# An FFT filter with a gated FFN on one Trainium2 core: the transformed rows placed at another address, 160 bytes past the input weights mod 256

## The chip, the cores and the metric

The kernel runs on one core of one Trainium2 chip. The metric is the device time of one execution in microseconds (us), the median of repeated runs; shorter is better. A profiled execution of the same kernel gives the rows of the profile and the trace.

## The reference

Eight sequences of 3136 rows with 256 features each are filtered along the sequence in the frequency domain and then go through a gated feed-forward layer:

```python
X = np.fft.rfft(x, axis=1)                       # x: 8 x 3136 x 256
y = np.fft.irfft(X * (filt_r + 1j * filt_i), n=3136, axis=1)

h = np.maximum(y @ w_in, 0.0)                    # 256 -> 1024
conv_out[s] = sum over k of conv_w[k] * h[s + k - 1]   # 3 taps along the rows
gate = 1.0 / (1.0 + np.exp(-conv_out))
return (h * gate) @ w_out                        # 1024 -> 256
```

## The kernel before, in words

**Forward part.** A sequence of 3136 = 112 x 28 rows is transformed in stages of small float32 matmuls: `first` (line 323), a transpose through TensorE (line 334), `second` (lines 346 and 349), the filter on VectorE and GpSimd (lines 358 to 362) and `third` (line 233), whose result goes to a scratch tensor in HBM. The last inverse stage, `last_stage` (line 215), reads it back as `br` and leaves four 128x112 blocks in PSUM. `last_out` turns these into two tiles: ScalarE copies the rounded value (line 146) into `y0`, VectorE writes what the rounding left over (line 149) into `y1`. These two are the high and the low *part* of the transformed rows, in a type (float32r) that TensorE takes at a higher rate than float32.

**The tiles the change touches.** `y_slices` makes, for each sequence, two tiles `y0` and `y1` of 128 partitions x 2 x (3136 + 2) elements. Index 1 is the *half*: features 0 to 127 and 128 to 255. The two extra columns hold the zero rows at the ends, which the convolution needs. The tiles of even sequences lie in the pool `y_even`, allocated from the right end of SBUF, those of odd sequences in `y_odd`, allocated from the left behind the pool `rest`. The pool `rest` has a tile `pad` of 192 elements that nobody reads or writes; all it does is to move what is allocated behind it.

**Feed-forward part.** The schedule is written by hand: a loop over 448 steps (28 chunks of 896 rows x 8 blocks of 128 hidden features x 2 halves of a chunk of 448 rows). In each step TensorE does `inner`: 450 columns of rows (448 and one more on either side) against one block of the input weights, in three products (high weights x high rows on line 177, high x low on line 178, low x high on line 179) for each of the two halves of the features, so six matmuls of 128x450 in the order 177, 178, 179 (half 0), 177, 178, 179 (half 1). Each has its own weight load of 128x128 from `wi`. The rows are the *moving* operand, streamed through the array. Behind it comes `project` of an earlier step: 9 or 12 matmuls of 128x256 (lines 498 to 500), with the gated features `g` as the loaded weights and the output weights `wo` as the moving operand. ScalarE does relu, scaling, sigmoid and rounding (lines 465, 467, 477, 146), VectorE the taps and the product (472, 473, 478), GpSimd the low part of `g` (152). In some steps, 14 to a sequence, a piece of the next sequence's last inverse stage is put between.

**Where the operands lie** (byte offsets in a partition, and the same mod 256):

| operand | offset | mod 256 |
|---|---|---|
| `wi` high, low | 1696, 9888 | 160, 160 |
| `wo` high, low | 18080, 26272 | 160, 160 |
| `g`, all buffers | 117472 and on | 224 |
| odd `y0` / `y1`, half 0 | 60064 / 85184 | 160 / 192 |
| odd `y0` / `y1`, half 1 | 72616 / 97736 | 168 / 200 |
| even `y0` / `y1`, half 0 | 179104 / 204224 | 160 / 192 |
| even `y0` / `y1`, half 1 | 191656 / 216776 | 168 / 200 |

A block of weights starts at a multiple of 512 bytes from the tile's start, and a piece of 448 rows at a multiple of 1792 = 7 x 256, so these residues hold for every matmul of `inner`. Counted from the weights, the six matmuls read their rows at 0, 32, 0 (half 0) and 8, 40, 8 (half 1).

Of the kernel before, what the change touches and what calls it, by code (L numbers as in the profile page):

```python
# [9 lines left out]
F32 = mybir.dt.float32  # L10
F32R = mybir.dt.float32r
# [5 lines left out]
S = 3136  # L17
# [5 lines left out]
KT = D // 128  # L23
# [101 lines left out]
def tile_fft_filter_gated_ffn(  # L125
# [67 lines left out]
    ys, yps = {}, []  # L193
# [6 lines left out]

    def y_slices(b, sl):
        if sl.start == 0:
            ys[b] = [yps[b % 2].tile([128, KT, S + 2], F32R, name=f"y{h}") for h in range(2)]
            for t in ys[b]:
                nc.gpsimd.memset(t[:, :, 0:1].bitcast(F32), 0.0)
                nc.gpsimd.memset(t[:, :, S + 1:S + 2].bitcast(F32), 0.0)
        return (t[:, :, 1:S + 1].rearrange("p k (a c) -> p k c a", c=N2)[:, :, sl] for t in ys[b])
# [10 lines left out]
    def last_out(b, c):  # L218
        yh, yl = y_slices(b, slice(c, c + 2))
        pv = lasts.pop((b, c))[:, 0:4 * N1].rearrange("p (k c a) -> p k c a", c=2, a=N1)  # L220
        hi_act(yh, pv)
        lo_dve(yl, pv, yh)

    NP = 14
    rest = ctx.enter_context(tc.tile_pool(name="rest", bufs=3))
    i1_sb = rest.tile([120, G, 112], F32, name="i1_sb", bufs=1)
    rest.tile([128, 192], F32, name="pad", bufs=1)
    parts = {}

    def third(b, p, ps):  # L230
# [366 lines left out]
```

## Time and profile before

| | |
|---|---|
| time of three runs | 1559.26, 1559.91, 1562.10 us; median 1559.91 |
| profiled execution | 1559.94 us, span of its instructions 1558.2 us |
| granted TensorE clock | 0.999 |
| TensorE busy | 1537.8 us (99%) |
| VectorE, ScalarE, GpSimd busy | 1297.0, 1245.0, 703.0 us |

In the profile PE is TensorE's matmuls and PEld its weight loads, DVE is VectorE, ACT ScalarE, POOL GpSimd. A float32 matmul appears as two instructions, one for each of its passes, while a float32r one appears once. Matmuls are pipelined, so the duration shown of one is longer than the distance from its start to the next one's start; both are used below, and kept apart.

### The profile page before, as it was taken

Reading aid. Unit: us, or ns where it says so; the run is one execution under the profiler, and the core shown is the slowest. Engines: PE = TensorE matmul, PEld = TensorE weight load, DVE = VectorE, ACT = ScalarE, POOL = GpSimd, SP = SyncE. Lnnn points to the kernel's source line nnn. Section 1 sums busy time; section 2 is a strip of 40 time slices with the busy share of each in tenths; the row PEclk is TensorE's granted clock in tenths of the full one; section 3 lists DMA queues with packets and bytes.
Section 4 is the critical chain, followed back from the end, with each engine's and each line's share of the span. In section 5 each row is a group of like instructions: output and inputs, shape, how many; then the busy total and the mean of one; then the engine's idle time right before and its main releaser. Section 6 shows DMA issues by size and latency. Waiting matters only on the chain.

```text
span 1558.2 us, 27801 instructions
## 1 busy us (share of the span) xinstructions
PE 1537.8 (99%) x10320; PEld 1418.2 (91%) x10320; DVE 1297.0 (83%) x1978; ACT 1245.0 (80%) x2274; POOL 703.0 (45%) x625
## 2 busy tenths in 40 slices
PE   8999999998999999999999999999999999999998
PEld 7787778877999999999999999999999999999998
DVE  3888888788888888888888888888888888888887
ACT  5655555566888888888888888888888888888887
POOL 3455555533444444444444444444444434444444
PEclk9999999999999999999999999999999999999999
DMA  9855555452111011111111011111011110100001
GB/s 236 261 179 168 172 169 164 137 148 78 33 52 48 31 47 48 49 49 47 48 42 36 27 53 52 44 48 48 31 48 42 49 54 27 46 25 25 24 25 48
DMA packets 89062, 115.24 MB, mean 74 GB/s; under 512 B 7400, under 2 KB 60168, under 8 KB 88928
## 3 DMA queue, kind: packets, MB, share of 16 engines
q1 hardware_dynamic: 74592, 87.77, 18.4%
q10 hardware_dynamic: 14336, 25.70, 5.8%
q8 instruction: 82, 1.34, 0.4%
q14 instruction: 52, 0.43, 0.1%
HBM read 62.06 MB, written 51.38 MB: 73 GB/s over the span
## 4 chain that ended last, share of the span: by engine, by line
PE 94%; DMA 2%; DVE 1%; ACT 1%; issue 0%; SPq 0%; POOL 0%; ACTq 0%; POOLq 0%; DVEq 0%
PE ps_h L178 12%; PE ps_h L179 12%; PE ps_h L177 11%; PE po L498 11%; PE po L500 11%; PE po L499 11%; PE ps L233 6%; PE ps_h L215 5%; PE pp L346 5%; PE ps L323 5%; PE ps L334 3%; DMA x<-in_x 1%; PE ps L215 1%; DVE y L149 1%; ACT y L146 0%; PE pp L349 0%
## 5 line engine op out<-in xcount | busy, mean ns | idle before, releaser
L152 POOL TENSOR_TENSOR g<-t,g 128x448 fp32r<-128x448 f32 x448 | 517.1, 1154 | 663.5 <-ACT g L146 259.3
L498 PE MATMUL po<-wo,g 128*128 128x256 f32 x1568 | 441.4, 282 | 0.0
L500 PE MATMUL po<-wo,g 128*128 128x256 f32 x1568 | 433.9, 277 | 0.4 <-POOL g L152 0.4
L499 PE MATMUL po<-wo,g 128*128 128x256 f32 x1568 | 433.4, 276 | 0.0
L472 DVE SCALAR_TENSOR_TENSOR t<-ps_h,cw,t 128x448 f32<-128x448 f32 x448 | 305.7, 682 | 85.6 <-ACT t L467 75.2
L178 PE MATMUL ps_h<-y,wi 128*128 128x450 f32 x896 | 330.3, 369 | 5.6 <-DVE y L149 5.6
L177 PE MATMUL ps_h<-y,wi 128*128 128x450 f32 x896 | 329.1, 367 | 3.3 <-DVE t L478 1.9
L179 PE MATMUL ps_h<-y,wi 128*128 128x450 f32 x896 | 328.8, 367 | 0.0
L473 DVE SCALAR_TENSOR_TENSOR t<-ps_h,cw,t 128x448 f32<-128x448 f32 x448 | 306.5, 684 | 16.0
L467 ACT ACTIVATE t<-ps_h,cw 128x448 f32<-128x448 f32 x448 | 284.8, 636 | 43.2 <-ACT ps_h L465 2.6
L498 PEld LDWEIGHTS po<-wo,g 128*128 128x128 f32 x1568 | 294.8, 188 | 7.1
L499 PEld LDWEIGHTS po<-wo,g 128*128 128x128 f32 x1568 | 294.3, 188 | 5.7
L500 PEld LDWEIGHTS po<-wo,g 128*128 128x128 f32 x1568 | 294.5, 188 | 0.6 <-POOL g L152 0.6
L465 ACT ACTIVATE ps_h<-ps_h 128x450 f32<-128x450 f32 x448 | 251.8, 562 | 32.9 <-PE ps_h L179 27.0
L478 DVE TENSOR_TENSOR t<-ps_h,t 128x448 f32<-128x448 f32 x448 | 275.3, 615 | 0.1
L477 ACT ACTIVATE t<-t 128x448 f32<-128x448 f32 x448 | 255.0, 569 | 12.4 <-DVE t L473 11.2
L146 ACT ACTIVATE g<-t 128x448 fp32r<-128x448 f32 x448 | 254.7, 568 | 0.2 <-DVE t L478 0.2
L362 POOL TENSOR_TENSOR z<-u,v 120x512 f32<-120x512 f32 x112 | 156.6, 1398 | 184.3 <-DVE v L360 154.1
L178 PEld LDWEIGHTS ps_h<-y,wi 128*128 128x128 f32 x896 | 168.3, 188 | 14.7 <-DVE y L149 7.9
L179 PEld LDWEIGHTS ps_h<-y,wi 128*128 128x128 f32 x896 | 168.3, 188 | 13.9
L177 PEld LDWEIGHTS ps_h<-y,wi 128*128 128x128 f32 x896 | 169.9, 190 | 11.7 <-DVE t L478 2.9
L149 DVE TENSOR_TENSOR y<-ps_h,y 128x448 fp32r<-128x448 f32 x98 | 103.1, 1053 | 75.3 <-ACT y L146 75.3
(62 smaller groups left out, 1661.6 us busy)
## 6 DMA issues: line engine op xcount, KB each, us to landing
x<-in_x SPq DMA_DIRECT2D x112, 224.0 KB, 2.9
b_dram<-sb ACTq DMA_DIRECT2D x112, 224.0 KB, 2.3
br<-b_dram SPq DMA_DIRECT2D x112, 224.0 KB, 2.6
out<-ot SPq DMA_DIRECT2D x27, 896.0 KB, 4.1
raw<-in_w_in SPq DMA_DIRECT2D x8, 256.0 KB
raw<-in_w_out SPq DMA_DIRECT2D x8, 256.0 KB
t_sb<-in_fr SPq DMA_DIRECT2D x15, 112.0 KB
t_sb<-in_fi SPq DMA_DIRECT2D x14, 112.0 KB
```

The costliest lines, as they stand in the source:

```text
L152: nc.gpsimd.tensor_tensor(out=dst, in0=src, in1=hi.bitcast(F32), op=ALU.subtract)
L177: nc.tensor.matmul(ps, lhsT=wh, rhs=rh, start=start, stop=False, **kw)
L178: nc.tensor.matmul(ps, lhsT=wh, rhs=rl, start=False, stop=False, **kw)
L179: nc.tensor.matmul(ps, lhsT=wl, rhs=rh, start=False, stop=stop, **kw)
L467: nc.scalar.activation(t, h[:, 1:SUB + 1], AF.Copy, scale=cw[:, 1, f:f + 1])
L472: nc.vector.scalar_tensor_tensor(out=t, in0=h[:, 0:SUB], scalar=cw[:, 0, f:f + 1], in1=t, op0=ALU.mult, op1=ALU.add)
L473: nc.vector.scalar_tensor_tensor(out=t, in0=h[:, 2:SUB + 2], scalar=cw[:, 2, f:f + 1], in1=t, op0=ALU.mult, op1=ALU.add)
L477: nc.scalar.activation(t, t, AF.Sigmoid)
L478: nc.vector.tensor_mul(t, h[:, 1:SUB + 1], t)
L498: nc.tensor.matmul(o, lhsT=gh[:, sl], rhs=wo[0][:, f], start=first, stop=False, skip_group_check=True)
L499: nc.tensor.matmul(o, lhsT=gh[:, sl], rhs=wo[1][:, f], start=False, stop=False, skip_group_check=True)
L500: nc.tensor.matmul(o, lhsT=gl[:, sl], rhs=wo[0][:, f], start=False, stop=last, skip_group_check=True)
```

## The change

The rows' tiles get a pitch of 3136 + 64 elements for a half (12800 bytes = 50 x 256, before 12552), so that both halves and both parts start at the same residue mod 256. The pool of either kind of sequence is moved by a further 40 elements (160 bytes): on the left through the tile `pad`, on the right through a new unused tile. All four starts of the even tiles and all four of the odd ones are now at 64 mod 256, which is 160 past the input weights' 160.

```diff
     def y_slices(b, sl):
         if sl.start == 0:
-            ys[b] = [yps[b % 2].tile([128, KT, S + 2], F32R, name=f"y{h}") for h in range(2)]
+            ys[b] = [yps[b % 2].tile([128, KT, S + 64], F32R, name=f"y{h}") for h in range(2)]
+            if b < 2:
+                yps[b].tile([128, 40], F32, name="pad_y")
...
     i1_sb = rest.tile([120, G, 112], F32, name="i1_sb", bufs=1)
-    rest.tile([128, 192], F32, name="pad", bufs=1)
+    rest.tile([128, 232], F32, name="pad", bufs=1)
```

No instruction is added, removed or moved: on every engine the same instructions stand in the same order with the same waits, and only operand addresses differ. What lies behind `pad` moves along: the forward part's `z`, `sb`, `turn1`, `eye`, `s2`, `a`, `u`, `v` and the filter tiles by 160 bytes, `br` to 64 mod 256 (from 160). `wi`, `wo`, `m2`, `i1`, `s1`, `x` and `turn0` keep their addresses, and the feed-forward part's `t`, `g` and `ot` keep theirs mod 256 (224).

## Prediction

> **What bounds the kernel now.** The page first: whose time is the kernel's time. The rows are the span, part 1 (busy time) and part 4 (the chain of work that ended last, by engine).
>
> ```profile
> span 1558.2 us, 27801 instructions
> PE 1537.8 (99%) x10320; PEld 1418.2 (91%) x10320; DVE 1297.0 (83%) x1978; ACT 1245.0 (80%) x2274; POOL 703.0 (45%) x625
> ...
> PE 94%; DMA 2%; DVE 1%; ACT 1%; issue 0%; SPq 0%; POOL 0%; ACTq 0%; POOLq 0%; DVEq 0%
> ```
>
> TensorE is the kernel: 94% of the chain. The span is 1558.2 us, and the profiled execution's own time 1559.94, so 1.7 us lie around it; the median of the runs, 1559.91, is the same number. I sum against 1559.9. Next, by stretch: columns are the stretch, its length, then busy time of PE, PEld, DVE, ACT and POOL, granted clock, DMA share, GB/s.
>
> ```profile
> 0.00:365.00 365.00, 356.96 (x2132) 285.86 (x2132) 287.90 (x421) 219.45 (x379) 182.44 (x147) 1.00 0.62 180
> 365.00:1558.20 1193.20, 1180.82 (x8188) 1132.37 (x8188) 1009.08 (x1558) 1025.52 (x1895) 520.58 (x478) 1.00 0.13 41
> 380.00:960.00 580.00, 576.98 (x4026) 554.37 (x4025) 497.53 (x764) 504.97 (x931) 252.94 (x235) 1.00 0.14 44
> ```
>
> The feed-forward part is 1193 of 1558 us, at full clock, and PE is busy for 577 of 580 us. ScalarE comes next with 505 of 580, or 87%, so PE could get some 12% faster there before another engine is last. Hence a matmul that starts sooner shortens the end directly. Now the matmuls themselves, one step in the timeline (start, duration):
>
> ```profile
> 1001.69 0.37 PE L177 MATMUL ps_h<-y,wi 128*128 128x450 f32 x1
> 1001.90 0.36 PE L178 MATMUL ps_h<-y,wi 128*128 128x450 f32 x1
> 1002.10 0.37 PE L179 MATMUL ps_h<-y,wi 128*128 128x450 f32 x1
> 1002.30 0.36 PE L177 MATMUL ps_h<-y,wi 128*128 128x450 f32 x1
> 1002.51 0.37 PE L178 MATMUL ps_h<-y,wi 128*128 128x450 f32 x1
> 1002.72 0.36 PE L179 MATMUL ps_h<-y,wi 128*128 128x450 f32 x1
> 1002.92 0.28 PE L498 MATMUL po<-wo,g 128*128 128x256 f32 x1
> ...
> 1004.28 0.37 PE L177 MATMUL ps_h<-y,wi 128*128 128x450 f32 x1
> ```
>
> Six matmuls of 450 columns take 1.23 us, 205 ns from start to start; the twelve of 256 columns behind them 1.36 us, 113 ns each. Nothing stands between. So only the pace of a matmul can change the time here, and the change touches an operand of just the 450-column ones.
>
> **Does the address set that pace?** The same step in the list by line (duration ns min/median/max), each row restricted to one instruction; the order is 177, 178, 179 of half 0, then of half 1.
>
> ```profile
> L177 PE MATMUL ps_h<-y,wi x1: 367/367/367, 1001.7 to 1001.7; 128*128 128x450 f32 x1
> L178 PE MATMUL ps_h<-y,wi x1: 365/365/365, 1001.9 to 1001.9; 128*128 128x450 f32 x1
> L179 PE MATMUL ps_h<-y,wi x1: 367/367/367, 1002.1 to 1002.1; 128*128 128x450 f32 x1
> L177 PE MATMUL ps_h<-y,wi x1: 363/363/363, 1002.3 to 1002.3; 128*128 128x450 f32 x1
> L178 PE MATMUL ps_h<-y,wi x1: 369/369/369, 1002.5 to 1002.5; 128*128 128x450 f32 x1
> L179 PE MATMUL ps_h<-y,wi x1: 365/365/365, 1002.7 to 1002.7; 128*128 128x450 f32 x1
> ```
>
> With distances from the weights of 0, 32, 0, 8, 40, 8 bytes the durations are 367, 365, 367, 363, 369, 365. Lines 177 and 179 stream the very same rows, line 178 the low part. The shape, type and work are equal, and the two halves differ by 4 ns on lines 177 and 178 in opposite directions. What differs is the address (and, for the last, which operand is loaded next). Over the whole run it holds:
>
> ```profile
> L177 PE MATMUL ps_h<-y,wi x896: 363/367/579, 365.1 to 1545.1; 128*128 128x450 f32 x180
> L178 PE MATMUL ps_h<-y,wi x896: 365/369/579, 367.3 to 1545.3; 128*128 128x450 f32 x180
> L179 PE MATMUL ps_h<-y,wi x896: 360/367/579, 367.6 to 1545.5; 128*128 128x450 f32 x180
> ```
>
> 3 x 896 = 2688 matmuls, whose minimum is the fast position and whose median is the slow one on lines 177 and 178. The rows begin at seven places of each tile, 1792 bytes apart, and the blocks of weights 512 apart, and neither widens the two values: what matters, matters mod 256 or less.
>
> **How much is there to win or lose?** A matmul that streams unhindered is the lower end. The float32 passes give its price by column:
>
> ```profile
> L233 PE MATMUL ps<-z,i_sb x436: 377/378/470, 29.0 to 362.6; 120*112 120x256 f32 x146
> L346 PE MATMUL pp<-a,s_sb x208: 591/594/690, 23.1 to 360.2; 112*120 112x512 f32 x104
> L500 PE MATMUL po<-wo,g x1568: 276/276/384, 380.5 to 1553.8; 128*128 128x256 f32 x196
> ```
>
> (591 - 378) / 256 = 0.832 ns a column, and 378 - 256 x 0.832 = 165 ns of fixed latency. The float32r columns go at about twice that pace: 256 of them take 276, where 165 + 256 x 0.416 = 271.5 would be unhindered, an excess of 4.5 ns. For 450 columns it would be 165 + 187 = 352. The six positions average (367+365+367+363+369+365)/6 = 366, an excess of 14 ns, three times as much. Over 2688 matmuls that is 37.6 us: all that the address could win, with an end at 1522. Upward there is no row that bounds it; the worst position, 369, is 3 ns above the mean, or 8.1 us over all.
>
> [...]
>
> **The change part by part.** *New pitch and pads of the rows' tiles.* All six positions now read rows at one residue, 64 mod 256, 160 past the weights. The misaligned starts (168 and 200, not multiples of 16 or 32) are gone, and so is the shift of 32 between the parts. 64 isn't among the residues before, nor is 160 among the distances, so I bound the new duration: 352 from below (no hindrance), 369 as the worst seen, and from above by as much again as the mean is now hindered, 366 + 14 = 380 (+37.6 us, 1597.5). The row that is nearest in kind is line 178, half 0, at 192, the only one of the four starts that, like 64, is a multiple of 64: 365, and its successor starts 0.20 us later (1001.90 to 1002.10), where the slow 369 is followed after 0.21. The lowest row is 363, on line 177, which now also has no neighbour at another residue. I take 364, between the two: 2 ns below the mean of 366, and since durations exceed the distance between starts by a fixed amount (366 - 205 = 161), 2 ns of duration are 2 ns of time. 2688 x 2 ns = 5.4 us less, 1554.5.
>
> *Forward part, moved by 160 bytes.* Its float32 passes stream at half the pace. Line 233 loads its weights `i1` from four residues mod 256 (448 bytes a slice) against one residue of `z`, and minimum and median of 436 are 377 and 378: no address effect to 1 ns. I take nothing. If 1 ns appeared on each of its 2132 matmuls, it would be 2.1 us either way.
>
> *Writes of the rows.* ScalarE and VectorE write them in a stride of 112 bytes:
>
> ```profile
> L146 ACT ACTIVATE y<-ps_h x98: 1002/1058/1099, 389.6 to 1392.6; 128x448 fp32r<-128x448 f32 x98
> L149 DVE TENSOR_TENSOR y<-ps_h,y x98: 981/1056/1083, 390.6 to 1393.7; 128x448 fp32r<-128x448 f32 x98
> ```
>
> These hide under PE's stream (ScalarE has 13% left). Only at the seven borders between sequences, and in the 14 pieces before the feed-forward part, does TensorE wait for such a pair. Were they 10% slower, 21 x 0.2 us = 4 us at most, of which I take none: the stride stays and only the start moves.
>
> *What the new tiles cost:* nothing, since nobody touches the pads. The sum is 1559.9 - 5.4 = 1554.5.
>
> **The rivals.**
>
> *Most of the hindrance goes (faster, by far).* The 256-column matmuls read `wo` at 160 while `g` is loaded from 224, a distance of 192 bytes, near to the new 160; their excess is 4.5 ns in place of 14. If distance to the operand being loaded is what counts, the new one may come down to that: 2688 x 9.5 = 25.5 us, 1534.4. Against it: line 179 of half 1 is followed by a load of `g`, at a distance of 200, and it still takes 365. Also, in the 256-column stream a weight load may simply be the bound (PEld is busy for 554 of 580 us), so its 4.5 may tell nothing of conflicts. 0.21.
>
> *The new distance is a bad one (slower).* If the hindrance comes from rows and weights meeting in the same part of the memory while a load runs, one common residue makes all six matmuls meet it in the same way. Now they are spread over 363 to 369, then all could sit at 369 or beyond: 2688 x 3 = +8.1 us, 1568.0. It decides from a duration of 367.2 on (366 + 3.1 us / 2688). For it: 32 to 40 bytes moves it by 4 ns, so the dependence is steep, and a place picked among such values is above the mean about as often as below. Against it: half of the six positions, those on a shifted half, lose an 8-byte offset. 0.30.
>
> *Nothing happens.* The differences among the six may come from their place in the order (which product follows which) rather than from the address, and the mean stays: 1559.9. [...] 0.17.
>
> **How the numbers follow.** The forecast, a small gain near the lowest of the starts seen, has 0.32. What a measurement of this kernel can tell from no change is about 0.2%, or 3.1 us. Faster by more: the forecast and the first rival, 0.32 + 0.21 = 0.53. Same: 0.17. Slower: 0.30. Range: down to 1532, which takes in 1534.4 with the 2 us of the forward part, and leaves out the complete disappearance; up to 1571, the third of the bad cases beyond 369 left out. Cases of both signs hold most of the chance; the forecast's own range, durations from 361 to 365.5, is 1546.5 to 1558.6.
>
> **What would show it.** Right: lines 177, 178 and 179 each with one duration in the trace after (minimum and median equal, save where the next load is of another kind), near 364, and six starts of a step in 1.22 us in place of 1.23; lines 498 to 500 still 276; line 233 still 378. The first rival would show 357 and a step of 1.17 us, the second 369 or more and 1.25 us. Wrong in its ground would be: line 177 still with two values though its addresses are alike, or time that moved while these rows stood still, in the forward part (0 to 365) or as waits for lines 146 and 149.

## The result and the profile after

The changed kernel takes 1579.14 us (median of 4 runs, 1578.21 to 1579.42) against 1560.24 before: a ratio of 1.0119, 95% interval 1.0101 to 1.0136. It is 18.9 us slower, where 5.4 us less was forecast. The profiled execution took 1579.2 us.

The page after, its span, busy times and chain:

```profile
span 1577.4 us, 27801 instructions
PE 1557.2 (99%) x10320; PEld 1435.8 (91%) x10320; DVE 1295.9 (82%) x1978; ACT 1245.7 (79%) x2274; POOL 703.5 (45%) x625
...
PE 94%; DVE 2%; DMA 2%; ACT 1%; issue 0%; POOL 0%; SPq 0%; ACTq 0%; POOLq 0%; DVEq 0%
```

Nothing has taken TensorE's place: it is busy for 19.4 us more (1557.2 - 1537.8) in a span 19.2 us longer, and the others are as they were. So the same matmuls run slower. The first and last start of line 177 say where:

```profile
L177 PE MATMUL ps_h<-y,wi x896: 363/369/579, 367.3 to 1564.4; 128*128 128x450 f32 x180
```

From 367.3 to 1564.4 are 1197.1 us, before 365.1 to 1545.1, 1180.0: 17.1 of the 19.2 us lie in the feed-forward part, 2.2 ahead of it. The groups of the page, each with its count, busy time and mean duration, show which matmuls (lines 177 to 179 are the same in both kernels; `project` moved from 498-500 to 500-502). Before:

```profile
L498 PE MATMUL po<-wo,g 128*128 128x256 f32 x1568 | 441.4, 282 | 0.0
L500 PE MATMUL po<-wo,g 128*128 128x256 f32 x1568 | 433.9, 277 | 0.4 <-POOL g L152 0.4
L499 PE MATMUL po<-wo,g 128*128 128x256 f32 x1568 | 433.4, 276 | 0.0
...
L178 PE MATMUL ps_h<-y,wi 128*128 128x450 f32 x896 | 330.3, 369 | 5.6 <-DVE y L149 5.6
L177 PE MATMUL ps_h<-y,wi 128*128 128x450 f32 x896 | 329.1, 367 | 3.3 <-DVE t L478 1.9
L179 PE MATMUL ps_h<-y,wi 128*128 128x450 f32 x896 | 328.8, 367 | 0.0
```

After:

```profile
L500 PE MATMUL po<-wo,g 128*128 128x256 f32 x1568 | 445.2, 284 | 0.0
L501 PE MATMUL po<-wo,g 128*128 128x256 f32 x1568 | 438.9, 280 | 0.0
L502 PE MATMUL po<-wo,g 128*128 128x256 f32 x1568 | 437.7, 279 | 0.4 <-POOL g L152 0.4
...
L178 PE MATMUL ps_h<-y,wi 128*128 128x450 f32 x896 | 332.0, 371 | 5.6 <-DVE y L149 5.6
L177 PE MATMUL ps_h<-y,wi 128*128 128x450 f32 x896 | 333.3, 372 | 3.2 <-DVE t L480 1.8
L179 PE MATMUL ps_h<-y,wi 128*128 128x450 f32 x896 | 331.2, 370 | 0.0
```

The sum of the 256-column products goes from 1308.7 to 1321.8 us (+13.1), that of the 450-column ones from 988.2 to 996.5 (+8.3). Durations overlap, so the two don't add up to the 17.1 us. Time from each start to TensorE's next start does: summed over the trace from the first line 177 on, it goes from 546.5 to 557.9 us for the 256-column products (+11.4) and from 561.8 to 567.5 for the 450-column ones (+5.7), and stays at 80.4 for the rest. So two thirds of the loss fall on the 256-column products, **whose operands `wo` and `g` have kept their residues mod 256**. One step in the timeline after:

```profile
808.33 0.37 PE L177 MATMUL ps_h<-y,wi 128*128 128x450 f32 x1
...
809.57 0.28 PE L500 MATMUL po<-wo,g 128*128 128x256 f32 x1
...
810.27 0.28 PE L500 MATMUL po<-wo,g 128*128 128x256 f32 x1
...
810.95 0.37 PE L177 MATMUL ps_h<-y,wi 128*128 128x450 f32 x1
```

Six products of 450 columns take 1.24 us (before 1.23) and twelve of 256 columns 1.38 (before 1.36). The first six of the twelve take 0.70 us, 117 ns each, the last six 0.68, 113 ns, which is the pace before. The delay sits right behind the 450-column products and wears off: averaged over all groups behind `inner`, the first five take 115 to 120 ns and the rest 113 to 114, where before all took 113 to 114 (the eleventh alone averages 117 in both). And the six, one by one:

```profile
L177 PE MATMUL ps_h<-y,wi x1: 373/373/373, 808.3 to 808.3; 128*128 128x450 f32 x1
L178 PE MATMUL ps_h<-y,wi x1: 369/369/369, 808.5 to 808.5; 128*128 128x450 f32 x1
L179 PE MATMUL ps_h<-y,wi x1: 372/372/372, 808.7 to 808.7; 128*128 128x450 f32 x1
L177 PE MATMUL ps_h<-y,wi x1: 369/369/369, 809.0 to 809.0; 128*128 128x450 f32 x1
L178 PE MATMUL ps_h<-y,wi x1: 369/369/369, 809.2 to 809.2; 128*128 128x450 f32 x1
L179 PE MATMUL ps_h<-y,wi x1: 366/366/366, 809.4 to 809.4; 128*128 128x450 f32 x1
```

All six read rows at one residue, with one distance to `wi`, and still show 373 to 366 ns: what was named ahead as a sign that the ground of the forecast is wrong.

### The profile page after: what moved, and what is told of

It reads as the page before. It is cut to its first block, busy times and chain, and to the rows that moved or that the text cites. A ratio compares the mean times of both kernels' runs of the same rounds, so it can differ in the third digit from the quotient of the medians.

```text
span 1577.4 us, 27801 instructions
## 1 busy us (share of the span) xinstructions
PE 1557.2 (99%) x10320; PEld 1435.8 (91%) x10320; DVE 1295.9 (82%) x1978; ACT 1245.7 (79%) x2274; POOL 703.5 (45%) x625
## 4 chain that ended last, share of the span: by engine, by line
PE 94%; DVE 2%; DMA 2%; ACT 1%; issue 0%; POOL 0%; SPq 0%; ACTq 0%; POOLq 0%; DVEq 0%
PE ps_h L178 12%; PE ps_h L179 12%; PE ps_h L177 12%; PE po L500 11%; PE po L501 11%; PE po L502 11%; PE ps L325 6%; PE ps L235 6%; PE ps_h L217 5%; PE pp L348 5%; PE ps L336 3%; PE ps L217 1%; DMA x<-in_x 1%; DVE y L149 1%; ACT y L146 0%; DMA t_sb<-in_fr 0%
```

## The experiments

Theory A: the rows' distance from the weights decides. Rival B: the moved tiles of the forward part. Rival C: that the parts and halves now share one residue. Rival D: the rows' own residue, whatever the weights'. Ratios are against the kernel before, run beside.

**Rows alone, forward part alone.** `rows_only`, against the kernel before, with the pads in the rows' pools instead of `rest` (the second on the left keeps `t` and `g` at 224):

```diff
+            if b < 2:
+                yps[b].tile([128, (0, 40)[b]], F32, name="pad_first")   # odd only
-            ys[b] = [yps[b % 2].tile([128, KT, S + 2], F32R, name=f"y{h}") for h in range(2)]
+            ys[b] = [yps[b % 2].tile([128, KT, S + 64], F32R, name=f"y{h}") for h in range(2)]
+            if b < 2:
+                yps[b].tile([128, 40], F32, name="pad_y")
```

> The rows lie as in the changed kernel (64 mod 256, 160 past the weights), and the forward part's own tiles stay where they were before. Theory A (the rows' distance from the weights costs the time): 1579, as the changed kernel. Rival B (the moved tiles of the forward part, or what follows from them): near 1560.

`fwd_only`, against the kernel before:

```diff
+            if b < 2:
+                yps[b].tile([128, (0, 24)[b]], F32, name="pad_first")   # odd only
...
-    rest.tile([128, 192], F32, name="pad", bufs=1)
+    rest.tile([128, 232], F32, name="pad", bufs=1)
```

> The forward part's tiles are moved by 160 bytes, the rows keep their old pitch and residues mod 256 (the odd ones lie 256 bytes further). Theory A: 1560, no difference to before. Rival B: near 1579.

Measured: rows alone 1576.74 us, ratio 1.010 (1.008 to 1.012); forward part alone 1561.18, ratio 0.9999 (0.9989 to 1.0008). The groups of `rows_only`, then of `fwd_only`:

```profile
L504 PE MATMUL po<-wo,g 128*128 128x256 f32 x1568 | 445.2, 284 | 0.0
L177 PE MATMUL ps_h<-y,wi 128*128 128x450 f32 x896 | 333.3, 372 | 3.2 <-DVE t L484 1.9 <-ACT y L146 1.2
```

```profile
L501 PE MATMUL po<-wo,g 128*128 128x256 f32 x1568 | 441.4, 281 | 0.0
L177 PE MATMUL ps_h<-y,wi 128*128 128x450 f32 x896 | 329.0, 367 | 3.4 <-DVE t L481 1.9 <-ACT y L146 1.2
```

All six groups of the first repeat the changed kernel's to 0.2 us, those of the second the kernel before's to 0.1. Rival B is out. The writes of the rows at their new address can't be it either: ScalarE and VectorE write rows in 98 of the 448 steps only, while in the changed kernel the 249 groups behind `inner` with no such write beside them are slow as well (115 to 120 ns in their first five, before 113), and line 146 takes 1055 ns for a write in the changed kernel, against 1058 before. The 2.2 us ahead of the feed-forward part are not settled: its first matmul starts at 366.9 in `fwd_only` and 365.5 in `rows_only`, but kernels with the forward part untouched spread over 364 to 367.5.

**The weights move, or all move.** `shift_all` is the changed kernel with 24 more elements ahead of `wi`, and the right-hand pad cut from 40 to 16:

```diff
+    wc.tile([128, 24], F32, name="pad_w")
     wi = [wc.tile([128, KT, FF], F32R, name=f"wi{h}") for h in range(2)]
...
-                yps[b].tile([128, 40], F32, name="pad_y")
+                yps[b].tile([128, (16, 40)[b]], F32, name="pad_y")
```

> The changed kernel with weights, rows, gated tiles and the forward part's left-hand tiles all moved on by 96 bytes: rows at the old residue 160, still 160 past the weights. Theory A: 1579, since only the distance counts. Rival D (the absolute residue of the rows counts): back to about 1560.

`wi_moved` is the changed kernel with `wi` alone at the rows' residue:

```diff
+    wc.tile([128, 40], F32, name="pad_w")
     wi = [wc.tile([128, KT, FF], F32R, name=f"wi{h}") for h in range(2)]
+    wc.tile([128, 24], F32, name="pad_wo")
     wo = [wc.tile([128, NF, D], F32R, name=f"wo{h}") for h in range(2)]
```

> The changed kernel with its rows where they are, and the input weights alone moved to them: distance 0 from the rows, while output weights and gated tiles keep their residues. If the distance to the input weights decides: the durations and the time of all_0, about 1569. If the rows' distance to the gated tiles or the output weights decides, or their own residue: 1579.

Measured: 1580.35 us, ratio 1.012 (1.0105 to 1.0135), with all of it moved by 96 bytes; 1565.59, ratio 1.0029 (1.0019 to 1.0038), with `wi` moved to the rows. So the rows' own residue (rival D) doesn't matter, while where they lie to the other operands does: `wi` moved by 160, with nothing else at another residue, wins back 14 of 19 us. That it is their distance to `wi` alone isn't shown, since this move also changes how `wi` lies to `wo` and `g`. The groups of `wi_moved`:

```profile
L503 PE MATMUL po<-wo,g 128*128 128x256 f32 x1568 | 443.2, 283 | 0.0
L505 PE MATMUL po<-wo,g 128*128 128x256 f32 x1568 | 437.9, 279 | 0.4 <-POOL g L152 0.4
L504 PE MATMUL po<-wo,g 128*128 128x256 f32 x1568 | 435.5, 278 | 0.0
L178 PE MATMUL ps_h<-y,wi 128*128 128x450 f32 x896 | 329.0, 367 | 5.7 <-DVE y L149 5.7
L177 PE MATMUL ps_h<-y,wi 128*128 128x450 f32 x896 | 328.8, 367 | 3.3 <-DVE t L483 1.9 <-ACT y L146 1.2
L179 PE MATMUL ps_h<-y,wi 128*128 128x450 f32 x896 | 326.7, 365 | 0.0
```

Its 450-column products take 984.5 us, less than before's 988.2; its 256-column ones 1316.6, 7.9 more than before. A good place for the one isn't a good place for the other. The expectation was the durations and the time of `all_0` (below), which has the same distance 0; the time came out 3 us under its 1569, and the durations differ.

**The distance, all rows at one residue.** `all_N` are `rows_only` with other pads (in elements, first and behind on the left, behind on the right): 0 and 16, 16 for distance 0; 16 and 0, 0 for 64; 32 and 48, 48 for 128; 48 and 32, 32 for 192; 56 and 24, 24 for 224. One of them:

```diff
+            if b < 2:
+                yps[b].tile([128, (0, 16)[b]], F32, name="pad_first")   # all_64, odd only
-            ys[b] = [yps[b % 2].tile([128, KT, S + 2], F32R, name=f"y{h}") for h in range(2)]
+            ys[b] = [yps[b % 2].tile([128, KT, S + 64], F32R, name=f"y{h}") for h in range(2)]
```

> The new pitch, but both parts and both halves at 160 mod 256, distance 0 from the weights; the forward part as before. Theory A (the distance decides, and 160 is a bad one): clearly under 1579; at the old durations for distance 0, 367 ns, about +2.7 us on before, so 1560 to 1565. Rival C (it is the uniformity that costs: all streams and loads now walk in one phase): about 1579, or more.

> New pitch, all rows 64 past the weights, forward part as before. Theory A (the distance decides): a value of its own, anywhere from 1550 to 1585; it need not be above 1560. Rival C (uniformity costs by itself, and 160 adds to it): no uniform distance is under the 1569 of distance 0.

> New pitch, all rows 128 past the weights. If the pattern repeats every 128 bytes or less, as all_0, 1569. If it repeats only every 256, a value of its own. Rival C: 1569 or more.

> New pitch, all rows 192 past the weights, the distance that the 256-column products have to their own weights. My first rival of the prediction, turned round: if that distance is a good one, the 450-column products come down to 195 to 200 ns and the run to 1535 to 1550. Otherwise near its neighbour, 160: 1570 to 1580.

> New pitch, all rows 224 past the weights, 32 short of them. Theory A with a slow dependence: between all_192 and all_0's 1569. Rival C: 1569 or more.

**The distance, with the old shape.** `old_shape_N` keep the old pitch and the old shifts (32 between the parts, 8 between the halves), moved on by N with pads of N/4 elements in front on the left and (256 - N)/4 behind on both sides:

```diff
+            if b < 2:
+                yps[b].tile([128, (0, 16)[b]], F32, name="pad_first")   # old_shape_64, odd only
             ys[b] = [yps[b % 2].tile([128, KT, S + 2], F32R, name=f"y{h}") for h in range(2)]
+            if b < 2:
+                yps[b].tile([128, 48], F32, name="pad_y")
```

> Old pitch and old shifts between parts and halves, moved on by 64: distances 64, 96, 72, 104. The uniform 64 cost 0.75%. If the old shape is what keeps the time low wherever it lies: 1560 to 1566. If distance counts as much in the old shape as in the uniform one: 1572.

> Old pitch and old shifts, moved on by 128: distances 128, 160, 136, 168. The uniform 128 was the best uniform one (0.32%). If the old shape gains at every distance: 1556 to 1561, the best of all. If the old place was only a lucky one: 1565 or more.

> The old pitch and the old shifts of 32 and 8 bytes, all of it moved on by 160: distances 160, 192, 168, 200. Theory A (distance decides; 160 and 192 are the two worst): 1575 to 1581. Rival C (uniformity costs, distance matters little): 1560 to 1563.

> Old pitch and shifts, moved on by 192: distances 192, 224, 200, 232. If the uniform and the old shape follow one curve over distance (192 was the worst uniform one at 1.22%): 1575 or more. If each arrangement has a curve of its own, as old_shape_128 against all_128 suggests: anything, 1560 to 1585, with no bound from the uniform row; under 1557 it would be a better kernel than both.

> Old pitch and shifts, moved on by 224: distances 224, 0, 232, 8. One curve over distance (uniform 224 cost 0.61%, uniform 0 0.45%): 1568 to 1572. A curve of its own for each arrangement: not bound by that, 1560 to 1585; under 1557 it would be a better kernel than both.

Measured, ratio to before (95% interval):

| distance | all rows at one residue | old shape |
|---|---|---|
| 0 | 1.0045 (1.003 to 1.006) | 1 (the kernel before) |
| 64 | 1.0075 (1.006 to 1.009) | 1.0078 (1.0063 to 1.0093) |
| 128 | 1.0032 (1.0019 to 1.0045) | 1.0139 (1.0122 to 1.0155) |
| 160 | 1.010 (1.008 to 1.012), `rows_only` | 1.0027 (1.0018 to 1.0037) |
| 192 | 1.0122 (1.0107 to 1.0137) | 1.0085 (1.0067 to 1.0102) |
| 224 | 1.0061 (1.0044 to 1.0078) | 1.0066 (1.0051 to 1.0081) |

In the old shape the distance in the table is that of the high part of half 0; the other three lie 32, 8 and 40 further. No curve over this one distance serves both columns: 128 is the best in one and the worst in the other, 160 nearly the reverse. So Theory A falls in its simple form: at 160 the old shape takes 1565.47 us, 11 less than the uniform one, and under the 1575 to 1581 that it expected. Rival C expected 1560 to 1563 there, and falls by `old_shape_128`, which isn't uniform and is slower than any uniform one (in its strict form, no uniform distance under 1569, `all_128` at 1566.62 is barely against it). `all_0` at 1568.88 lies between the two expectations, 1560 to 1565 and 1579, and meets neither. Nor does each product go by its own distance: line 177 of half 1 reads at distance 8 in the kernel before and in `halves_apart` (below), with a median of 363 ns in the one and 372 in the other. My guess for distance 192 (1535 to 1550, if that is a good one) came out at 1581.18.

**Half the shape.** `parts_apart` has the new pitch with the low part 32 behind, `halves_apart` the old pitch with both parts at 160:

```diff
-            ys[b] = [yps[b % 2].tile([128, KT, S + 2], F32R, name=f"y{h}") for h in range(2)]
+            ys[b] = []
+            for h in range(2):
+                ys[b].append(yps[b % 2].tile([128, KT, S + 64], F32R, name=f"y{h}"))   # halves_apart: S + 2
+                if b < 2 and h == 0:
+                    yps[b].tile([128, 8], F32, name="pad_mid")   # halves_apart: 56
+            if b < 2:
+                yps[b].tile([128, 8], F32, name="pad_y")
```

> The new pitch (both halves at one residue), but the low part 32 bytes behind the high one as before: rows at 160 and 192, distances 0 and 32, forward part as before. If the shift of 8 bytes between the halves is what helped the old layout: 1567 to 1570, as all_0. If the shift of 32 between the parts helped: 1560.

> The old pitch (halves 8 bytes apart, 160 and 168), but both parts at the same residue: distances 0 and 8. If the shift between the parts helped the old layout: 1567 to 1570. If the shift between the halves helped: 1560.

Measured: 1564.2 us, ratio 1.0023 (1.0013 to 1.0033), and 1571.23, 1.0062 (1.0046 to 1.0078). The shift between the parts wins back half of what `all_0` lost (1560 or 1567 to 1570 were expected); the shift between the halves, alone, doesn't help. Neither alone gives before's time: the two interact. On line 177 of half 1 the shift of 8 turns a median of 364 ns (`all_0`) into 372 (`halves_apart`), but with the shift of the parts beside it 361 (`parts_apart`) into 363 (the kernel before).

**Two paces of one product.** `all_192` shows the 256-column products best. Their first stretch below follows a piece of the last inverse stage (line 221), the second follows `inner`; the shape, the residues and the order are the same:

```profile
1006.26 0.28 PE L506 MATMUL po<-wo,g 128*128 128x256 f32 x1
...
1007.28 0.28 PE L506 MATMUL po<-wo,g 128*128 128x256 f32 x1
...
1008.62 0.28 PE L504 MATMUL po<-wo,g 128*128 128x256 f32 x1
...
1009.68 0.37 PE L177 MATMUL ps_h<-y,wi 128*128 128x450 f32 x1
```

Nine distances take 1.02 us in the first (113 ns) and 1.06 in the second (118 ns), to the end of the step. So the pace of these products isn't set by their own addresses alone: it differs with the matmuls ahead, 113 or 118 ns. Which pace follows depends on the rows' layout, since before the change it was 113 behind `inner`. In `rows_only` it is the other way round. Behind `inner` the pace is back at 113 from the sixth product on, and behind a piece of the last inverse stage it stays slow:

```profile
1001.77 0.28 PE L506 MATMUL po<-wo,g 128*128 128x256 f32 x1
...
1002.83 0.28 PE L506 MATMUL po<-wo,g 128*128 128x256 f32 x1
```

Nine distances take 1.06 us here (118 ns); over all 97 such groups most places take 117 to 118 (in the changed kernel too), where the kernel before has 113 from the fifth product on. Neither these products' operands nor those of the piece lie at another residue than before the change: only the rows do, which were streamed ahead of the piece. So the slow pace seems to outlast the eight float32 passes between. The next rows are also written while this group runs; that these writes have a part in it isn't ruled out.

**Shorter weight loads.** If the streams are held up by the weight loads beside them, halving the loads should halve the hold-up. `short_before` and `short_after` leave out half of the hidden features (64 of each block of 128; `t` and both parts of `g` are cut to 64 partitions in the same way):

```diff
+HF = 64
...
-        ps = ps_h.tile([128, 512], F32, name="ps_h")[:, 0:SUB + 2]
-        fs = slice(128 * f, 128 * f + 128)
+        ps = ps_h.tile([128, 512], F32, name="ps_h")[0:HF, 0:SUB + 2]
+        fs = slice(128 * f, 128 * f + HF)
...
-            nc.tensor.matmul(o, lhsT=gh[:, sl], rhs=wo[0][:, f], start=first, stop=False, skip_group_check=True)
+            nc.tensor.matmul(o, lhsT=gh[:, sl], rhs=wo[0][0:HF, f], start=first, stop=False, skip_group_check=True)
```

> The old layout, with half of the hidden features left out: each block of input weights is loaded with 64 columns in place of 128, and all that follows works on 64 partitions; number, order and streamed columns of the matmuls stay. [...]

> The same cut (half of the hidden features left out, loads of 64 columns in the 450-column products) in the changed layout. If the weight loads are what the rows meet: starts 197 to 200 ns apart, and the distance to the cut kernel in the old layout about half of 19 us. If the rows' address acts without the loads: 19 us slower than the cut kernel in the old layout.

Measured, one run each: 1722.83 and 1705.94 us, both much slower, so the totals tell nothing of this: at each change between blocks of 128x64 and 64x128 the next start comes some 86 ns later than before (290 against 205 ns into `project`, 202 against 116 out of it). Inside a group the starts can be read, in `short_before` and then in `short_after`:

```profile
1001.50 0.37 PE L178 MATMUL ps_h<-y,wi 128*64 128x450 f32 x1
...
1002.33 0.37 PE L179 MATMUL ps_h<-y,wi 128*64 128x450 f32 x1
```

```profile
1002.31 0.37 PE L178 MATMUL ps_h<-y,wi 128*64 128x450 f32 x1
...
1003.12 0.36 PE L179 MATMUL ps_h<-y,wi 128*64 128x450 f32 x1
1003.41 0.38 PE L500 MATMUL po<-wo,g 64*128 64x256 f32 x1
```

In the changed layout the distances fall from 207 to 202 ns (0.81 us over four); over all steps the first of the four takes 209 and the other three 200, near the 197 to 200 expected of a load that counts (207 less half of the 14 ns that the forecast estimated as the excess is 200). In the old one they don't fall, with 208 ns (0.83 over four) against 205. Inconclusive, then: halving the loads changes the pace, and turns the order of the two layouts round, but the hold-up isn't in proportion to the load.

## Why the prediction was wrong

**What bounds the kernel** held: TensorE's stream, 94% of the chain before and after, with no other engine last, and the address of an operand alone changes the time (1.0119). That no instruction moved, that pads cost nothing and that the forward part's move costs nothing (`fwd_only`, 0.9999) held too.

**The step that failed** is "the row that is nearest in kind is line 178, half 0 [...] 365". It takes each of the six durations for a property of that matmul's own address, and from it 2688 products at 364 ns, 5.4 us less. Measured were 370.7 (996.5 us over 2688), 5.7 us more from start to start. `all_0`, with all rows at the one residue 160, gives the six in order:

```profile
L177 PE MATMUL ps_h<-y,wi x1: 367/367/367, 805.2 to 805.2; 128*128 128x450 f32 x1
L178 PE MATMUL ps_h<-y,wi x1: 364/364/364, 805.4 to 805.4; 128*128 128x450 f32 x1
L179 PE MATMUL ps_h<-y,wi x1: 367/367/367, 805.6 to 805.6; 128*128 128x450 f32 x1
L177 PE MATMUL ps_h<-y,wi x1: 364/364/364, 805.8 to 805.8; 128*128 128x450 f32 x1
L178 PE MATMUL ps_h<-y,wi x1: 367/367/367, 806.0 to 806.0; 128*128 128x450 f32 x1
L179 PE MATMUL ps_h<-y,wi x1: 369/369/369, 806.2 to 806.2; 128*128 128x450 f32 x1
```

The fast place on line 178 is 364 here with distance 0, as it was 365 with distance 32, and the fast place on line 177, half 1, stays 364 without its shift of 8. So the pattern that I read as an effect of 32 and 8 bytes comes out much the same without those shifts. But it isn't a fixed property of the places either. The median durations over all steps, in ns:

| place | before | `all_0` | `halves_apart` | `wi_moved` |
|---|---|---|---|---|
| 177, half 0 | 367 | 367 | 367 | 363 |
| 178, half 0 | 365 | 364 | 364 | 367 |
| 179, half 0 | 367 | 367 | 367 | 364 |
| 177, half 1 | 363 | 364 | 372 | 367 |
| 178, half 1 | 369 | 367 | 370 | 364 |
| 179, half 1 | 365 | 369 | 369 | 363 |

The shift of 8 between the halves, alone, makes line 177 of half 1 slower by 8 ns (`all_0` to `halves_apart`). In `all_0` and `wi_moved` all rows lie at distance 0 from `wi`, and the fast and the slow places have changed round. So in these runs addresses and order act together: neither a product's own distance nor its place by itself gives the duration (line 177 of half 1 takes 363 ns in the kernel before and 372 in `halves_apart`, both at distance 8). My third rival was half right with the place in the order, and drew the wrong end from it: that the time would stay. The 4 ns between the two halves of line 178, taken for an effect of the address, were no argument against it, as these two stand at different places, second and fifth of the six.

**The term that was put at nothing** is the 256-column products, by the sentence that "the change touches an operand of just the 450-column ones". They took 13.1 us of added duration, 11.4 us from start to start, two thirds of the loss. In `all_0` they outweigh a gain: its 450-column groups sum to 987.6 us (329.3 + 328.7 + 329.6, before 988.2), and yet it is 0.45% slower, as this group shows best, against 441.4 before (the three sum to 1317.3, against 1308.7):

```profile
L501 PE MATMUL po<-wo,g 128*128 128x256 f32 x1568 | 446.4, 285 | 0.0
```

**The rival on the slow side** had the sign, and its price of +3 ns on 2688 matmuls, 8.1 us, meets the 8.3 us of duration in the 450-column groups. That is in part luck: from start to start it is 5.7 us, since a nanosecond of duration was not quite one of time here. Its picture, all six alike at 369, was not right: they range from 366 to 373. **The first rival** (the distance of 192 as a good one, 1534) fell with `all_192`, 1581.18 us, and with it the rule that the 256-column products' small excess tells of a good distance: their pace depends on what runs ahead of them. **Nothing happens** fell with `wi_moved`: moving the loaded operand, with rows, `wo` and `g` in place, changes the time by 14 us.

**The range** left 1579 out because it had no term for the 256-column products: the 450-column ones alone, 5.7 us, would have ended at 1565.6, within it. **The price of all that could be won**, 37.6 us down to 352 ns, was not borne out: the fastest place in any of these arrangements has a median of 361. And the base was off: of the fifteen arrangements of rows and weights timed, the one before is the fastest. So a move from it that isn't aimed by a measurement was likely to lose, and the 53% for a gain were not earned by anything in the profile.

**What stays open** is the mechanism. Shown: the time depends on where the rows lie to the weights (`rows_only`, `shift_all`, `wi_moved`), on how the four row streams differ among themselves (`parts_apart`, `halves_apart`), and on what ran ahead of a group of matmuls (the 120 ns that wear off to 113 within a group, and the two paces, 113 and 118 ns, in `all_192`). Not separated: the rows' distance to `wi` from the distances of both to `wo` and `g`. That streams and weight loads hit the same part of the memory at the same moment is a guess that would fit all three; no run shows it, the halved loads did not bear it out cleanly, and which part of the address counts was not found. No arrangement beat the kernel before.

## What to carry to other kernels

In this TensorE-bound kernel, whose matmuls follow each other without a gap, the address mod 256 of a streamed operand against that of the loaded one moved the time by 0.2 to 1.4%, all of it loss against the kernel before (a further 256 bytes for the odd rows, in `fwd_only`, cost nothing: 0.9999), two thirds of it in the changed kernel through later matmuls whose own operands stayed put. Durations of single matmuls at different places in the sequence didn't tell what an address would give at all of them (364 ns read off, 370.7 measured): the layout has to be timed as a whole. The kernel before was the fastest of fifteen layouts; that it came to this through measured variants, as its unused tile `pad` suggests, no run shows. Either way, an edit that moves tiles in a kernel like this is best laid out so that the residues stay, and a small loss after one is looked for there first.

## What the runs showed of the hardware

- The same 256-column float32r product, with the same residues, runs at 113 or at 118 ns from start to start in one execution, by what ran before it (`all_192`).
- Moving weights, rows and gated tiles together by 96 bytes changes nothing against the changed kernel (1580.35 against 1579.14 us); moving the input weights alone by 160 changes 0.9%.
- With 450 columns the forecast's estimate of an unhindered duration, 352 ns (worked out from the rows of lines 233 and 346), was not reached in any arrangement: the best, `wi_moved`, has a mean of 366 ns (984.5 us over 2688).
- In `rows_only` the slow pace of the 256-column products, 118 ns, is found behind eight float32 passes whose operands have the residues of the kernel before, which has 113 there; that the rows' writes beside them have a part in it isn't ruled out.
- Matmuls of 128x64 and 64x128 blocks in turn start later at each change: line 500 starts 0.29 us behind line 179 in `short_after`, against 0.20 to 0.21 us with all blocks 128x128.
- From start to start a float32r product of 256 columns takes 113 ns (line 498) and a float32 pass of 256 columns 215 (line 233), in the kernel before.
